# Threshold attention and SwiGLU on one core: one 130-column matmul for the last keys of both heads, score tiles with one user each at the end, stores on two queues

## The chip, the cores and the metric

The kernel runs on one core of a Trainium2 chip. A core has a matrix engine (TensorE, PE in the profile; its weight loads are PEld), a vector engine (VectorE, DVE), a scalar engine for activations (ScalarE, ACT), a general engine (GpSimd, POOL) and a queue engine (SyncE, SP) that here only issues transfers. They run side by side and wait for one another through semaphores. PE writes to PSUM, 8 banks of 128 partitions by 512 fp32 numbers; ACT and DVE read it from there; POOL does not. The metric is the time of one execution on the device in microseconds; the kernel before has a median of 575.13 us over six runs (574.01 to 576.0).

## The reference

Attention over 8 batches, 8 heads, 576 positions, head size 64, in which a score counts only if it lies within tau of the maximum of its row; then a gated feed-forward layer over the 4608 rows of 512.

```python
scores = scale * np.matmul(q, k.transpose(0, 1, 3, 2))
thresh = np.max(scores, axis=-1, keepdims=True) - tau
scores = np.where(scores >= thresh, scores, -1000000000.0)
scores = scores - np.max(scores, axis=-1, keepdims=True)
attn = np.exp(scores)
attn = attn / (np.sum(attn, axis=-1, keepdims=True) + 1e-09)
x = np.matmul(attn, v)                      # then heads side by side: 4608 x 512
...
rms = np.sqrt(np.mean(x * x, axis=-1, keepdims=True) + 1e-06)
xn = x / rms * rms_g
g = xn @ w_gate                             # 512 x 1536
silu = g * (1.0 / (1.0 + np.exp(-g)))
val = xn @ w_val
return (silu * val @ w_out).astype(np.float32)
```

## The kernel before

**Chunks and steps.** 128 query rows are a chunk. A batch of 576 rows gives four main chunks ("m"), and the 64 rows left over of two batches make one tail chunk ("v"): 36 chunks. A step is one chunk with one pair of heads, four steps a chunk, 144 in all. In a step PE computes the scores of both heads against 576 keys (line 566, into the two score tiles `s_ps[0]` and `s_ps[1]`, each of two PSUM banks), DVE copies them to `ssb` and takes the row maximum (line 589), POOL makes the threshold (line 596), ACT and POOL turn them into weights `wsb` (lines 607 to 645), and a transposing transfer on SP's queue (line 674; the first 16 steps go through PE, line 659) brings them as `wt`, nine blocks of 128 keys: four whole ones of head 0, one with the last 64 keys of head 0 and the first 64 of head 1, four of head 1. The sum over the values (`emit_av`, line 682, matmul at 696) takes two steps at a time: for each pair of heads, 5 matmuls a head, each of 65 columns, 64 of the values and one of ones for the row's sum of weights. The mixed block is used by both heads; the value tile `va` has rows of zeros there (entries 8 and 9, set at lines 270 and 271). In a tail chunk the upper and the lower 64 rows belong to two batches, so every matmul is made twice, with 64 columns of weights.

**The feed-forward layer.** DVE divides by the sum of weights (lines 712, 713) into `xsb`; ACT, POOL and a transposing transfer give the normalized, transposed chunk `xnT`. The chunks go through the layer in 12 groups (SIZES: four of two chunks, six of four, two of two). A group has 12 blocks of 128 hidden columns. For each, PE makes two products with the weights, g (line 790) and v (line 795), four matmuls each, of 512 columns in a group of four chunks and of 256 in a group of two; ACT takes tanh of g (line 804), DVE makes silu (line 807, frees g's tile) and the gate with v (line 812, `hf`, frees v's tile). Then the output sums: 12 matmuls of 512 columns a chunk. In eleven groups they come after the blocks, in two parts of six (line 849). In the last group (STREAMED = 1) they run between the blocks: one accumulation per chunk stays open over all 12 blocks, and each block adds two matmuls (line 829), planned OUT_LAG = 3 blocks behind its products. ACT evicts a finished sum to `osb` (line 863), in the last group DVE evicts the second chunk (line 861), and SP stores it (line 868; line 872 for a tail chunk).

**PSUM.** `ring` has four tiles of one bank and, as entries 4 to 7, the halves of the two score tiles: 4 and 5 are halves of `s_ps[0]`, 6 and 7 of `s_ps[1]` (line 207). Entries 4 to 7 join the ring only after the last scores have been read (`opens`, line 952). The framework puts waits between instructions that touch the same tile; a half of a score tile is the same tile as the other half.

**What sets the order.** Every piece of work is an `Op` with an engine, a planned cost (`COST`, line 16), a priority and what it needs. `order_ops` (line 42) plays them through with these costs, picks for each engine what can start first, gives out ring entries (those free first), and so fixes the order of each engine's instructions and the tiles they use. The costs decide the order alone; the chip then runs each engine's list in that order.

Of the kernel before, what the change touches and what calls it, by code (L numbers as in the profile page):

```python
# [13 lines left out]
SEM = 160.0  # L14
SLACK = 0.0
COST = dict(
    s_main=932.0, s_virt=900.0, tr_qk=530.0, tr4=230.0, tr_full=440.0, av_main=320.0, av_virt=500.0, ffn4=216.0, warm=3500.0,
    ttr=690.0, evac_qk=600.0, evac_half=380.0, evac_kt=350.0, prelu=700.0, exp2=1250.0, exp1=690.0, exp0=690.0,
    mask_d=750.0, mask_g=1740.0, take_g=1300.0, trw=510.0, evac_w=450.0, evac_wp=900.0, rz=180.0, xmul=420.0, sq=800.0, xn=720.0,
    pool_tiny=270.0, pool_mean=800.0, pool_dma=850.0, cast_v=650.0, cast_vt=420.0, cast_w=720.0,  # L20
# [4 lines left out]


class Op:
    __slots__ = ("eng", "cost", "prio", "deps", "fn", "ring", "frees", "slot", "end", "start", "dma", "opens", "nring", "mode", "bulk", "release")

    def __init__(self, eng, cost, prio, deps, fn, ring=None, frees=None, dma=0.0, nring=1, mode=0, bulk=False):  # L30
        self.eng, self.cost, self.prio, self.fn = eng, cost, prio, fn
        self.deps = [d for d in deps if d is not None]
        self.ring, self.frees, self.dma = ring, frees, dma
        self.slot = self.end = self.start = None
        self.opens = ()
        self.nring = nring
        self.mode = mode
        self.bulk = bulk
        self.release = 0.0


def order_ops(ops, ring_sizes):


    import heapq

    ring_free = {r: [(0.0, i) for i in range(n)] for r, n in ring_sizes.items()}
    users = {}
    left = {}
    for i, o in enumerate(ops):  # L50
        left[i] = len(o.deps)
        for d in o.deps:
            users.setdefault(id(d), []).append(i)
    pending = {}
    for i, o in enumerate(ops):
        pending.setdefault(o.eng, [])
        if not left[i]:
            pending[o.eng].append(i)
    eng_free = {e: 700.0 for e in pending}
    dma_free = 0.0  # L60
    mode = 0
    out = []
    ready_at = {i: 0.0 for i in range(len(ops))}
    while len(out) < len(ops):
        best = None
        for e, lst in pending.items():
            if not lst:
                continue
            t0 = eng_free[e]
            cand = None  # L70
            for i in lst:
                o = ops[i]
                t = max(t0, ready_at[i])
                if o.ring is not None:
                    if len(ring_free[o.ring]) < o.nring:
                        continue
                    t = max(t, sorted(ring_free[o.ring])[o.nring - 1][0])
                other = e == "PE" and o.mode != mode
                t = max(t, o.release)
                if o.bulk:  # L80
                    t = max(t, dma_free - BACKLOG)
                k = (t + (BIAS if other else 0.0), o.prio, i)
                if cand is None or k < cand:
                    cand = k
            if cand is not None and (best is None or cand < best[0]):
                best = (cand, e)
        (t, _, i), e = best
        o = ops[i]
        cost = o.cost
        if e == "PE":  # L90
            if o.mode != mode:
                t -= BIAS
                cost += SWITCH
            mode = o.mode
        o.start = t
        if o.ring is not None:
            o.slot = []
            for _ in range(o.nring):
                got = min(ring_free[o.ring])
                ring_free[o.ring].remove(got)  # L100
                o.slot.append(got[1])
        eng_free[e] = t + cost
        if o.dma:
            dma_free = max(dma_free, t + 300.0) + o.dma
            o.end = max(dma_free, t + o.cost) + (LAT_TR if o.cost == COST["sp_tr"] else 2000.0)
        else:
            o.end = t + cost
        if o.frees is not None:
            ring_free["R"].append((o.end + SEM, o.frees[0].slot[o.frees[1]]))
        for slot in o.opens:  # L110
            ring_free["R"].append((o.end + SEM, slot))
        pending[e].remove(i)
        out.append(o)
        for j in users.get(id(o), []):
            u = ops[j]
            wait = 0.0 if u.eng == o.eng and not o.dma else SEM + (SLACK if u.eng == "PE" else 0.0)
            ready_at[j] = max(ready_at[j], o.end + wait)
            left[j] -= 1
            if not left[j]:
                pending[u.eng].append(j)  # L120
    return out
# [3 lines left out]
def kernel(  # L125
# [12 lines left out]
    nc = tc.nc  # L138
    B, H, S, D = q.shape
# [78 lines left out]
    def add(eng, cost, prio, deps, fn, **kw):  # L218
        o = Op(eng, cost, prio, deps, fn, **kw)
        ops.append(o)  # L220
        return o
# [455 lines left out]
            w_read[s] = t  # L677
            w_ready[s] = [t]

    V_AT = ((0, 2, 4, 6, 8), (9, 1, 3, 5, 7))  # L680

    def emit_av(s):

        ci, p1 = steps[s]
        kind, b, c = chunks[ci]
        hp = p1 // 2

        def fn(o):
            for i in range(2):
                w, p = wt[(s - 1 + i) % NWT], p1 - 1 + i  # L690
                for h in range(2):
                    at = (2 * i + h) * (D + 1)
                    rows = [(slice(0, 128), b % 2)] if kind == "m" else [(HALF[e], e) for e in range(2)]
                    for rs, vi in rows:
                        for j in range(5):
                            nc.tensor.matmul(ring[o.slot[0]][rs, at:at + D + 1], w[:, 4 * h + j, rs],  # L696
                                             va[vi][:, p, V_AT[h][j]], start=(j == 0), stop=(j == 4))

        bs = [b] if kind == "m" else [2 * b, 2 * b + 1]
        deps = w_ready[s - 1] + w_ready[s] + [x for bb in bs for i in range(2) for x in v_ready[bb, p1 - i]]  # L700
        o = add("PE", 2 * COST["av_main" if kind == "m" else "av_virt"], s + AV_PRIO, deps, fn, ring="R",
                mode=0 if kind == "m" else 3)
        for i in range(2):
            av_of[s - i] = [o]
            for bb in bs:
                last_av[bb, p1 - i] = last_av.get((bb, p1 - i), []) + [o]

        r = rz[len(half_ev) % 3]

        def half(_):  # L710
            o3 = ring[o.slot[0]][:, 0:4 * (D + 1)].rearrange("p (h d) -> p h d", d=D + 1)
            nc.vector.reciprocal(out=r, in_=o3[:, :, D])
            nc.vector.tensor_tensor(  # L713
                out=xsb[ci % 2][:, 256 * hp:256 * hp + 256].rearrange("p (h d) -> p h d", d=D),
                in0=o3[:, :, 0:D], in1=r[:, :, None].to_broadcast([128, 4, D]), op=ALU.mult)

        half_ev.append(add("DVE", COST["rz"] + COST["xmul"], s + HALF_PRIO, [o] + x_done.get(ci - 2, []), half,
                           frees=(o, 0)))
# [48 lines left out]
    def emit_ffn(slot, parts, ready_step, pace, streamed):  # L767
# [55 lines left out]
        if streamed:  # L823

            acc = None
            for fc, (hi, m_) in enumerate(hs):
                def omm(o, fc=fc, hi=hi, first=acc):
                    for j in range(len(parts)):
                        nc.tensor.matmul(ring[(first or o).slot[j]], hf[hi][:, 128 * j:128 * (j + 1)], wo[:, fc],  # L829
                                         start=(fc == 0), stop=(fc == NFC - 1))  # L830

                mo = add("PE", len(parts) * COST["ffn4"], st + dt * (fc + OUT_LAG), [m_] + wo_ld + outs[-1:], omm,
                         ring=None if acc else "R", nring=len(parts))
                acc = acc or mo
                outs.append(mo)
                hf_use[hi] = [mo]
        for j, (ci, _) in enumerate(parts):
# [24 lines left out]
                else:  # L862
                    nc.scalar.activation(out=osb[oi], in_=ring[mo.slot[at]], func=AF.Copy, scale=0.5)  # L863

            def store(o, oi=oi, kind=kind, b=b, c=c):
                if kind == "m":
                    dst = out[b * S:b * S + MAIN].rearrange("(si sc) d -> si sc d", sc=4)[:, c]
                    nc.sync.dma_start(out=dst, in_=osb[oi])
                else:
                    for e in range(2):  # L870
                        r0 = (2 * b + e) * S + MAIN
# [1 line left out]

            e = add("DVE" if late else "ACT", 690.0 if late else 620.0, pr - PUSH[0], [outs[-1], osb_use.get(oi)], ev,
                    frees=(mo, at))
            osb_use[oi] = add("SP", COST["sp"] if kind == "m" else 1100.0, pr, [e], store, dma=DMA_NS['out'])
        if not streamed:
            for hi, _ in hs:
                hf_use[hi] = list(outs)
# [69 lines left out]
        if step > 0:  # L949
            o.deps.append(s_of[int(step)])  # L950
    for h in range(2):
        ttr_of[len(steps) - 1, h].opens = (4 + 2 * h, 5 + 2 * h)
    seq = order_ops(ops, {"R": 4})
    global LAST_SEQ
    LAST_SEQ = seq
# [3 lines left out]


PACE = 13.0
NHF = 16
SIZES = (2, 2, 2, 2, 4, 4, 4, 4, 4, 4, 2, 2)
LAG = 16.0
LAT_TR = 3000.0
REL = (0.0, 0.0)
REL_N = (0, 0)
STREAMED = 1
OUT_LAG = 3.0
OUT_PART = 6  # L970
ELAG = 16.0
NELAG = 0
# [58 lines left out]
```

## Time and profile before

| | |
|---|---|
| median of six runs | 575.13 us |
| the profiled execution | 575.72 us |
| its span, first to last instruction | 574.0 us |
| PE busy | 559.9 us (98%) |
| DVE, ACT, POOL busy | 426.8, 459.8, 322.6 us |
| scores, line 566, main chunks | 1024 matmul records, 171.4 us busy |
| value sums, line 696 | 1580 matmul records, 56.4 us busy |
| stores of 256 KB from SP | 32, median 2.7 us to landing |
| granted PE clock, mean | 0.999 of full |

Times are microseconds from the span's start. Matmuls overlap in the pipeline, so the records of one group add up to more than the time it adds; the chain of waits gives the advance. A chain line has start, length and what ran then; "issue" is time in which an engine waited for nothing that the profile shows. A line of stretches gives, per engine, busy time and in brackets the number of instructions. A line of groups gives line, engine, operation, output and inputs with shapes, count, busy time, mean length in ns, idle time just before and what ended it.

### The profile page before, as it was taken

What the parts mean: (1) busy time and instruction counts of PE and PEld (TensorE: products, weight loads), DVE (VectorE), ACT (ScalarE), POOL (GpSimd) and SP (SyncE); (2) the same over time, 40 slices, a digit from 0 to 9 for tenths busy, and PEclk for the clock granted to TensorE, in tenths of its full rate; (3) what the DMA queues carried; (4) which work ended last, traced back from release to release, by engine and by line L of the source; (5) the groups of instructions that cost most, each with busy time, mean ns of one, the idle gap of its engine ahead of it and who ended that gap; (6) DMA issues with size and microseconds to landing.
All of it is one profiled execution on the core that took longest, in us unless ns stands there. A gap on an engine that the chain in (4) does not pass through costs nothing.

```text
span 574.0 us, 14110 instructions
## 1 busy us (share of the span) xinstructions
PE 559.9 (98%) x5160; PEld 333.0 (58%) x5160; DVE 426.8 (74%) x1093; ACT 459.8 (80%) x739; POOL 322.6 (56%) x462
## 2 busy tenths in 40 slices
PE   8999999999999999999999999999999999999995
PEld 4666776767757555555555455655555455544763
DVE  4898986868848688659975889578867886585543
ACT  4998898998969788889988997888978997883322
POOL 2377956875747456655765666665666665541000
PEclk9999999999999999999999999999999999999999
DMA  8999999868995679988887597966788544641111
GB/s 183 233 262 242 237 180 204 149 133 193 176 184 120 131 159 153 175 163 186 154 190 159 119 173 172 196 162 148 164 199 164 108 102 112 146 93 48 56 38 37
DMA packets 271173, 89.01 MB, mean 155 GB/s; under 512 B 253696, under 2 KB 263424, under 8 KB 271104
## 3 DMA queue, kind: packets, MB, share of 16 engines
q1 hardware_dynamic: 268448, 86.28, 70.8%
q0 software_dynamic: 1600, 1.57, 1.8%
q8 instruction: 40, 0.66, 0.5%
q10 hardware_dynamic: 1056, 0.26, 0.2%
q14 instruction: 29, 0.24, 0.1%
HBM read 37.75 MB, written 9.44 MB: 82 GB/s over the span
## 4 chain that ended last, share of the span: by engine, by line
PE 85%; DVE 4%; DMA 4%; issue 2%; ACT 2%; POOL 1%; SPq 1%; DVEq 0%; POOLq 0%; ACTq 0%
PE s_ps L566 26%; PE ring L795 14%; PE ring L849 14%; PE ring L790 14%; PE ring L696 7%; PE ring L302 2%; DMA qkn<-in_q_dram 2%; DVE ssb L589 2%; PE s_ps L790 1%; DMA wt<-wsb 1%; PE s_ps L795 1%; DMA stage<-in_moe_w_gate_dram 1%; PE s_ps L829 1%; PE ring L364 1%; PE s_ps L849 1%
## 5 line engine op out<-in xcount | busy, mean ns | idle before, releaser
L589 DVE CUSTOM_DVE_ANT_0 ssb<-s_ps,zrow 128x576 f32<-128x576 f32 x288 | 206.8, 753 | 60.8 <-PE s_ps L566 55.7
L607 ACT ACTIVATE ssb<-ssb,nth 128x576 f32<-128x576 f32 x224 | 165.6, 766 | 26.4 <-POOL nth L596 26.0
L566 PE MATMUL s_ps<-qkt 64*128 64x288 f32 x1024 | 171.4, 430 | 1.6 <-DVE mx L589 1.4
L566 PEld LDWEIGHTS s_ps<-qkt 64*128 64x128 f32 x1024 | 95.7, 186 | 56.0 <-DVE mx L589 14.2
L640 POOL TENSOR_SCALAR wsb<-ssb,nth 128x576 f16<-128x576 f32 x64 | 110.5, 1726 | 13.0 <-ACT osb L863 5.0
L790 PE MATMUL ring<-xnT,wg 128*128 128x512 f16 (+1 forms) x524 | 108.4, 329 | 0.2 <-DVE sl L807 0.2
L795 PE MATMUL ring<-xnT,wv 128*128 128x512 f16 (+1 forms) x520 | 107.5, 329 | 0.2 <-DVE xsb L713 0.2
L596 POOL TENSOR_SCALAR nth<-mx 128x2 f32<-128x2 f32 x144 | 31.6, 220 | 131.4 <-DVE mx L589 117.3
L614 ACT ACTIVATE wsb<-ssb 128x1152 f16<-128x1152 f32 x80 | 93.0, 1163 | 2.5 <-DMA wt<-wsb 0.2
L849 PE MATMUL ring<-wo,hf 128*128 128x512 f16 x384 | 89.3, 380 | 0.0
L804 ACT ACTIVATE th<-ring 128x512 f32<-128x512 f32 (+1 forms) x131 | 63.6, 487 | 31.4 <-PE ring L790 25.9
L645 POOL TENSOR_TENSOR wsb<-wsb,esb 128x576 f16<-128x576 f16 x64 | 81.8, 1278 | 9.8 <-ACT esb L626 5.0
L807 DVE SCALAR_TENSOR_TENSOR sl<-th,ring 128x512 f32<-128x512 f32 (+1 forms) x131 | 72.9, 556 | 15.8 <-ACT th L804 15.3
L812 DVE TENSOR_TENSOR hf<-ring,sl 128x512 f16<-128x512 f32 (+1 forms) x130 | 73.0, 562 | 13.1 <-PE ring L795 4.6
L795 PEld LDWEIGHTS <-wv 128*128 128x128 f16 x576 | 51.7, 98 | 43.8 <-issue 14.4
L790 PEld LDWEIGHTS <-wg 128*128 128x128 f16 x576 | 52.1, 98 | 40.7 <-issue 10.6
L849 PEld LDWEIGHTS <-hf 128*128 128x128 f16 x408 | 37.4, 98 | 47.0 <-issue 6.6
L696 PEld LDWEIGHTS <-wt 128*128 128x128 f16 (+1 forms) x1600 | 51.6, 100 | 19.9 <-issue 9.8
L696 PE MATMUL ring<-va,wt 128*128 128x65 f16 (+1 forms) x1580 | 56.4, 194 | 1.4 <-DMA wt<-wsb 1.4
L626 ACT ACTIVATE esb<-ssb,nth 128x576 f16<-128x576 f32 x64 | 49.2, 769 | 5.1 <-POOL nth L596 4.7
L611 ACT ACTIVATE wsb<-ssb 128x576 f16<-128x576 f32 x64 | 43.6, 682 | 1.7
L713 DVE TENSOR_TENSOR xsb<-ring,rz 128x256 f32<-128x256 f32 x71 | 30.2, 425 | 2.5
(65 smaller groups left out, 419.4 us busy)
## 6 DMA issues: line engine op xcount, KB each, us to landing
vst<-in_v_dram SPq DMA_DIRECT2D x32, 256.0 KB, 3.2
out_dram<-osb SPq DMA_DIRECT2D x32, 256.0 KB, 2.7
qkn<-in_k_dram SPq DMA_DIRECT2D x62, 128.0 KB, 3.3
qkn<-in_q_dram SPq DMA_DIRECT2D x56, 128.0 KB, 3.1
stage<-in_moe_w_gate_dram SPq DMA_DIRECT2D x12, 256.0 KB, 4.6
stage<-in_moe_w_val_dram SPq DMA_DIRECT2D x12, 256.0 KB, 4.6
wt<-wsb SPq DMA_TRANSPOSE x128, 3.1
wo<-in_moe_w_out_dram POOLq DMA_DIRECT2D x4, 384.0 KB, 6.8
```

Of the source, the lines that this page charges most:

```text
L566: nc.tensor.matmul(s_ps[h][rows, ROW_AT + n * part:ROW_AT + n * part + n], lhs(hs), kT[i][p][h][hs, n * part:n * part + n], start=True, st ...
L589: nc.vector.tensor_tensor_reduce(out=ssb[a][:, h], in0=s_ps[h][:, ROW_AT:ROW_AT + S], in1=zrow, scale=-1.0 / 8.0, scalar=3.0e38, op0=ALU.a ...
L607: nc.scalar.activation(out=ssb[a][:, h], in_=ssb[a][:, h], func=PRELU, scale=-1.0, bias=nth[m][:, h:h + 1], **PRELU_KW)
L614: nc.scalar.activation(out=wsb[s % NW], in_=ssb[a], func=AF.Exp)
L640: nc.gpsimd.tensor_scalar(out=wsb[s % NW][:, h], in0=ssb[a][:, h], scalar1=nth[m][:, h:h + 1], scalar2=None, op0=ALU.is_le)
L645: nc.gpsimd.tensor_tensor(out=wsb[s % NW][:, h], in0=wsb[s % NW][:, h], in1=esb[es], op=ALU.mult)
L696: nc.tensor.matmul(ring[o.slot[0]][rs, at:at + D + 1], w[:, 4 * h + j, rs], va[vi][:, p, V_AT[h][j]], start=(j == 0), stop=(j == 4))
L790: nc.tensor.matmul(ring[o.slot[0]][:, 0:n], wg[d][:, fs], xnT[slot][:, d, 0:n], start=(d == 0), stop=(d == 3))
L795: nc.tensor.matmul(ring[o.slot[0]][:, 0:n], wv[d][:, fs], xnT[slot][:, d, 0:n], start=(d == 0), stop=(d == 3))
L807: nc.vector.scalar_tensor_tensor(out=sl[i][:, 0:n], in0=th[i][:, 0:n], scalar=1.0, in1=ring[g.slot[0]][:, 0:n], op0=ALU.add, op1=ALU.mult)
L812: nc.vector.tensor_tensor(out=hf[hi][:, 0:n], in0=ring[vv.slot[0]][:, 0:n], in1=sl[i][:, 0:n], op=ALU.mult)
L849: nc.tensor.matmul(ring[(first or o).slot[0]], hf[hs[fc][0]][:, 128 * j:128 * (j + 1)], wo[:, fc], start=(fc == 0), stop=(fc == NFC - 1))
```

## The change

In the value sum the mixed block is multiplied once, with the values of both heads side by side, 130 columns, and opens the accumulation of both heads; four blocks of 65 columns a head follow. The loop over the halves of a tail chunk moves outside the loop over heads. The planned costs of the step fall from 320 to 310 and from 500 to 480.

At the end, only one half of each score tile joins the ring (entries 4 and 6). An `Op` can carry `pick`, the ring entries it may take; the first output sum of the last group has `pick = ACC`, entries 4 and 6, for its two chunks. OUT_LAG goes from 3 to 5. The store of the second chunk of the last group is issued by ACT. The planned latency of bulk loads gets a name of its own (LAT_LD) with the value it had.

```diff
-    V_AT = ((0, 2, 4, 6, 8), (9, 1, 3, 5, 7))
...
-                for h in range(2):
-                    at = (2 * i + h) * (D + 1)
-                    rows = [(slice(0, 128), b % 2)] if kind == "m" else [(HALF[e], e) for e in range(2)]
-                    for rs, vi in rows:
-                        for j in range(5):
-                            nc.tensor.matmul(ring[o.slot[0]][rs, at:at + D + 1], w[:, 4 * h + j, rs],
-                                             va[vi][:, p, V_AT[h][j]], start=(j == 0), stop=(j == 4))
+                rows = [(slice(0, 128), b % 2)] if kind == "m" else [(HALF[e], e) for e in range(2)]
+                for rs, vi in rows:
+
+                    at = 2 * i * (D + 1)
+                    nc.tensor.matmul(ring[o.slot[0]][rs, at:at + 2 * (D + 1)], w[:, 4, rs],
+                                     va[vi][:, p, 8:10].rearrange("p e d -> p (e d)"), start=True, stop=False)
+                    for h in range(2):
+                        for j in range(4):
+                            nc.tensor.matmul(ring[o.slot[0]][rs, at:at + D + 1], w[:, 5 * h + j, rs],
+                                             va[vi][:, p, 2 * j + h], start=False, stop=(h == 1 and j == 3))
+                        at += D + 1
...
-    s_main=932.0, s_virt=900.0, tr_qk=530.0, tr4=230.0, tr_full=440.0, av_main=320.0, av_virt=500.0, ffn4=216.0, warm=3500.0,
+    s_main=932.0, s_virt=900.0, tr_qk=530.0, tr4=230.0, tr_full=440.0, av_main=310.0, av_virt=480.0, ffn4=216.0, warm=3500.0,
...
-                    if len(ring_free[o.ring]) < o.nring:
+                    free = [f for f in ring_free[o.ring] if o.pick is None or f[1] in o.pick]
+                    if len(free) < o.nring:
                         continue
-                    t = max(t, sorted(ring_free[o.ring])[o.nring - 1][0])
+                    t = max(t, sorted(free)[o.nring - 1][0])
...
-                got = min(ring_free[o.ring])
+                got = min(f for f in ring_free[o.ring] if o.pick is None or f[1] in o.pick)
...
-                acc = acc or mo
+                if not acc:
+
+                    acc, mo.pick = mo, ACC
...
-                    nc.sync.dma_start(out=dst, in_=osb[oi])
+                    (nc.scalar if late else nc.sync).dma_start(out=dst, in_=osb[oi])
...
-            osb_use[oi] = add("SP", COST["sp"] if kind == "m" else 1100.0, pr, [e], store, dma=DMA_NS['out'])
+            late = late and kind == "m"
+            osb_use[oi] = add("ACT" if late else "SP", COST["sp"] if kind == "m" else 1100.0, pr, [e], store,
+                              dma=DMA_NS['out'])
...
-        ttr_of[len(steps) - 1, h].opens = (4 + 2 * h, 5 + 2 * h)
+        ttr_of[len(steps) - 1, h].opens = OPENS[h]
...
+ACC = (4, 6)
+OPENS = ((4,), (6,))
...
-OUT_LAG = 3.0
+OUT_LAG = 5.0
```

More of the change, by code (lines that the diff above doesn't have):

```diff
@@ L27 @@
 class Op:
-    __slots__ = ("eng", "cost", "prio", "deps", "fn", "ring", "frees", "slot", "end", "start", "dma", "opens", "nring", "mode", "bulk", "release")
+    __slots__ = ("eng", "cost", "prio", "deps", "fn", "ring", "frees", "slot", "end", "start", "dma", "opens", "nring", "mode", "bulk", "release", "pick")
     def __init__(self, eng, cost, prio, deps, fn, ring=None, frees=None, dma=0.0, nring=1, mode=0, bulk=False):
@@ L39, in __init__ @@
         self.release = 0.0
+        self.pick = None
 def order_ops(ops, ring_sizes):
@@ L104, in order_ops @@
             dma_free = max(dma_free, t + 300.0) + o.dma
-            o.end = max(dma_free, t + o.cost) + (LAT_TR if o.cost == COST["sp_tr"] else 2000.0)
+            o.end = max(dma_free, t + o.cost) + (LAT_TR if o.cost == COST["sp_tr"] else LAT_LD if o.bulk else 2000.0)
         else:
@@ L863, in ev, with store @@
                     nc.scalar.activation(out=osb[oi], in_=ring[mo.slot[at]], func=AF.Copy, scale=0.5)
-            def store(o, oi=oi, kind=kind, b=b, c=c):
+            def store(o, oi=oi, kind=kind, b=b, c=c, late=late):
                 if kind == "m":
                     dst = out[b * S:b * S + MAIN].rearrange("(si sc) d -> si sc d", sc=4)[:, c]
-                    nc.sync.dma_start(out=dst, in_=osb[oi])
+                    (nc.scalar if late else nc.sync).dma_start(out=dst, in_=osb[oi])
                 else:
@@ L965 @@
 LAT_TR = 3000.0
+LAT_LD = 2000.0
 REL = (0.0, 0.0)
```

## The prediction, written before the changed kernel ran

> **What bounds the kernel now.** I read the busy times first: PE is busy for 559.9 of 574.0 us, DVE for 74% and ACT for 80%, so what can be won is PE's 14.1 us of idle time, or PE work taken out. The second view is the busy time of each engine by stretch, cut where the instruction order of the changed program first departs (88 us), where idle time nearly ends (180 us) and where the last group of four chunks begins its output sums (524 us).
>
> ```profile
> core 0: us, PE busy (x) PEld busy (x) DVE busy (x) ACT busy (x) POOL busy (x), PEclk, DMA share, GB/s
> 0.00:88.00 88.00, 82.96 (x824) 56.97 (x825) 69.98 (x200) 72.51 (x115) 50.63 (x93) 1.00 1.01 223
> 88.00:180.00 92.00, 90.08 (x954) 61.84 (x953) 70.90 (x201) 80.97 (x138) 61.47 (x84) 1.00 0.87 168
> 180.00:524.00 344.00, 343.66 (x3102) 186.15 (x3099) 264.09 (x641) 292.13 (x455) 209.06 (x284) 1.00 0.72 150
> 524.00:574.00 50.00, 43.17 (x290) 28.10 (x288) 21.79 (x53) 14.17 (x34) 1.45 (x3) 0.99 0.14 46
> ```
>
> The reader is to see the first number after the length: PE idles 5.0 us at the start (there the order is unchanged), 1.9 us to 180, 0.3 us in the long middle, 6.8 us in the last 50. Only the last stretch is large, and the chain of waits says why:
>
> ```profile
> 524.37 10.37 PE ring L849 x48
> 534.74 0.03 ACTq L863
> ...
> 535.74 0.60 PE s_ps L790 x4
> ...
> 545.89 5.19 PE s_ps L849 x24
> 551.09 0.02 issue
> 551.11 0.61 ACT osb L863
> 551.72 0.04 issue
> 551.76 0.60 PE s_ps L795 x4
> ...
> 554.54 0.45 PE s_ps L829 x2
> 554.99 0.02 issue
> 555.01 0.39 ACT th L804
> ...
> 555.42 0.43 DVE sl L807
> ...
> 555.95 0.44 DVE hf L812
> 556.39 0.04 issue
> 556.43 0.59 PE s_ps L829 x2
> ```
>
> The chain leaves PE in the middle of the last group: tanh of one block waits for an output sum (L829), and the next output sum waits for that block's silu and gate. They share no data. They share the tile s_ps: the sums lie in one half of s_ps0 and of s_ps1, the block's two products in the other halves. The same pattern returns at 559.2 and 563.9. At 551.1 a product waits for an eviction of the neighbouring half, at 535.7 for a tanh.
>
> **The change, part by part.** The sum is made against the profiled execution, span 574.0 us, its time 575.72 us; the 1.72 us outside the span are left as they are.
>
> (a) The 130-column matmul. On the 128-row chunks a weighted sum of one head pair goes from 10 matmuls of 65 columns to 8 of 65 and one of 130, with one weight load less. There are 64 such steps with two pairs, 128 mergers. Price: one step of 20 advances the chain by 0.61 us (at 85.39 us and in most others), 30.5 ns each. No 130-column row exists. The nearest are the 128-column transposes, and above them the 256-column products (0.44 us for 4 in the chain, 109 ns):
>
> ```profile
> 53.89 0.50 PE ring L659 x9
> ```
>
> 0.50 / 9 is 55.6 ns. On a line from 65 columns at 30.5 ns to 128 at 55.6 ns, 130 columns take 56.4 ns; I take this, two columns from the nearer row. A merger saves 61.0 - 56.4 = 4.6 ns, 128 of them 0.6 us. Ends: 55.6 ns gives 0.7 us gained, 109 ns would give 128 x 48 ns = 6.1 us lost, which so near to the 128-column row I leave out. The Trainium skill, "TensorE: Matmul & The Clock Gate", section "Back-to-back issue gap", speaks against the change: in a stream of weight load and matmul pairs it gives a sustained spacing of about 81 ns at 128 columns, not the 56 ns of a lone gap. By that figure, as an estimate, a merger would lose 81 - 61 = 20 ns, 2.6 us over 128. The row above has a weight load before each of its matmuls and advances by 55.6 ns, so the sum goes by the row.
>
> In the 8 steps on the tail chunk, 40 matmuls of 128x64 become 36, and their order changes: all nine of one half of the partitions, then all nine of the other, where five and five alternated. The group of that form shows 320 matmuls in 7.1 us, 22 ns each, less than the 30.5 ns of a full one, so the halves overlap today. If they go on overlapping, nothing changes (the columns are the same). If the longer blocks end the overlap, a step takes 32 x 30.5 + 4 x 56.4 = 1.20 us instead of 0.89 us: 2.5 us lost in all. I take 0, since they now overlap across blocks of five pairs. Part (a): -0.6 us.
>
> (b) One user for each score tile, the group before the last. It now takes its products from the four ring tiles and one half of each score tile. In the program as built no product writes beside a half that is being read. From the end of the sums, 534.74, to 545.89 the chain shows 11.15 us; the work is 24 groups of four at 0.436 us (0.44 in the chain), 10.46 us. The difference, 0.69 us, goes. The tanh before 535.7 still waits for ACT's last eviction, but PE has three tile pairs to go on with, 2.6 us of work. Six tiles in place of eight are enough: from the start of a block's first product to the end of its gate is 2.0 to 2.4 us in this stretch. -0.7 us.
>
> (c, d) The last group. From 551.08 to PE's end at 569.39 are 18.31 us. The work is 24 x 0.436 + 24 output matmuls at 0.216 to 0.218 (1.31 us for 6) = 15.7 us. So 2.6 us are waits: 0.4 us at 551.1, and three times 0.73 us (1.44 us of the chain from 554.99 to 556.43, less the 0.87 us of two products done meanwhile, plus 0.16 us because the next L829 starts at 0.59 instead of 0.43). The sums now lie alone in their tiles, and products use the four ring tiles. A ring tile comes round after two blocks, 2 x 1.30 us of PE work, against the 2.0 to 2.4 us above, so no new wait there. Sums trail by five blocks (OUT_LAG 5): after the last product five pairs of output matmuls follow, 2.2 us, of which 1.7 us cover the last gate (0.2 drain + 0.42); at present three pairs do. New is one wait: the first sum needs both score tiles back, so the gate of block five. It is placed 13 groups, 5.67 us, into the stage; that gate ends 5.5 to 5.9 us in (start at 3.49 us, plus 2.0 to 2.4). Behind it all of PE is queued; cost 0 to 0.45 us with the 0.16 us restart, I take 0.1. -2.6 + 0.1 = -2.5 us.
>
> (e) The last store goes from SP's queue to ACT's. DVE's eviction, which starts at 569.41 and takes 0.69 us, ends at 570.10; SP issues that store only at 570.58, after its other one of 569.82:
>
> ```profile
> 570.58 0.33 SPq L868 DMA_DIRECT2D out_dram<-osb  x1
> ```
>
> On ACT nothing stands ahead of it (its eviction ends at 569.79) and nothing is queued behind. SP's first store was issued 0.03 us after its eviction; the same on ACT gains 0.45 us. The transfers then overlap more: the first took 2.1 us to landing, the second 2.5. If both share a fixed rate the gain is 0; if the second also takes 2.1 us it is 0.8; ACT's two loads at the start took 0.64 us to issue, which could cost 0.3. I take -0.45, ends -0.8 to +0.3. The Trainium skill, "DMA: Bandwidth & Descriptors", section "Issuing engines are not separate DMA queues", says that several issuers save only the sequencer's time to initiate. By it the gain would be the 0.33 us of the row, 0.1 us less than taken.
>
> (f) The order. The planned costs of L696's steps fall (320 to 310, 500 to 480), and from 88 us on 337 of PE's 652 steps stand elsewhere, by at most 8 places; SP's queue moves by up to 6. Both orders go 137 times from full-array work to scores and 104 times straight back, so the price of switching is the same. PE's idle 1.9 us in 88 to 180 can vanish or double: 0, ends -1.9 to +1.9.
>
> Sum: -0.6 - 0.7 - 2.5 - 0.45 = -4.25 us, a span of 569.75 us. The median of the runs, 575.13 us, is 0.6 us under the profiled 575.72; taken from it: **570.9 us**.
>
> **The rivals.**
> 1. The waits move instead of going. During the sums only four tiles serve the products, and DVE (0.42 + 0.42 us a block) can be late with them. For it: in the group before, DVE is busy 8.18 of 11.00 us, and the slack at the first sum is about nothing. Against: with sums a block costs PE 1.30 us and DVE 0.84. If the three waits stay, 2.2 us come back: 573.1 us.
> 2. The tail chunk's halves stop overlapping: +2.5 us, 573.4 us. For it: blocks of nine. Against: the 22 ns row.
> 3. Slower: the new order uses up PE's reserve in the middle. Between 180 and 524 us ACT is 85% and DVE 77% busy and PE idles 0.1%, because products stand ready between score steps. Scores wait for DVE already (in 88 to 180 the weight loads of L566 waited 2.9 us for it, 10 times). If the middle idled like that stretch, 2.1%, it would lose 7.2 - 0.3 = 6.9 us: 577.8 us. It decides from 1.2% of 344 us on, which eats the 4.25. Against: the displacements are small and the switches equal.
> 4. A milder form of 3, or several ends at once, leaves about 575.
>
> **How the numbers follow.** Forecast 0.66, own range 568.8 to 573.0 (the ends of the first sum's wait, e and f, about 0.4, 0.7 and 1.9 us, put together as squares: 2.1 us). Rival 1: 0.11, rival 2: 0.07, rival 4: 0.07, rival 3: 0.09. About 0.2%, 1.15 us, is what a measurement can tell. Faster is the forecast with rivals 1 and 2, less a little for their upper edges: 0.82; same 0.09, slower 0.09. The range of 568.8 to 574.0 leaves out rivals 3 and 4 and a little below.
>
> **What would show it.** In the profile after, the last group should have no pieces of ACT or DVE between L829's successors; output sums to PE's end about 15.8 us; the stretch before it 10.5 us; the last store on ACT's queue within 0.1 us of its eviction; L696's step of 18 at 0.59 us; PE idle of about 0.3 us in the middle. Wrong it is if the middle idles by several us, if the tail chunk's steps take 1.2 us, or if the first sum waits longer than 0.5 us.

## The result, and the profile after

The changed kernel takes 572.89 us (median of 40 runs, 570.62 to 576.55), the kernel before beside it 574.61 us (82 runs, 572.51 to 578.01). The ratio is 0.997, 95% interval 0.9961 to 0.998: 1.7 us faster, where 4.25 us were forecast. The profiled execution took 573.62 us, its span is 571.5 us. Two of the 21 executions of the kernel before in the first set of experiments took 1873 us; the ratios leave them out, and without them its median there is 574.83 us.

The busy time by stretch, in the columns of the prediction:

```profile
core 0: us, PE busy (x) PEld busy (x) DVE busy (x) ACT busy (x) POOL busy (x), PEclk, DMA share, GB/s
0.00:88.00 88.00, 82.64 (x803) 56.73 (x803) 69.79 (x199) 72.35 (x115) 50.43 (x92) 1.00 1.02 223
88.00:180.00 92.00, 90.20 (x938) 62.63 (x935) 71.86 (x203) 81.29 (x139) 63.05 (x86) 1.00 0.83 168
180.00:524.00 344.00, 343.70 (x2972) 188.10 (x2971) 264.54 (x640) 291.84 (x455) 207.23 (x282) 1.00 0.73 150
524.00:571.50 47.50, 43.09 (x295) 28.63 (x293) 21.77 (x53) 13.83 (x33) 1.44 (x3) 1.00 0.14 48
```

PE idles 5.4, 1.8, 0.3 and 4.4 us, where it was 5.0, 1.9, 0.3 and 6.8: the middle is as full as before, and the 4.4 us of the end are all behind PE's last matmul. So waits did go, and the rest of the gain must have been spent in work that counts as busy. The chain of waits shows where:

```profile
101.73 0.54 PE ring L794 x4
102.27 0.17 PE ring L695
102.45 0.16 PE ring L699 x5
102.60 0.03 PE ring L695
102.64 0.18 PE ring L699 x7
102.82 0.03 PE ring L695
102.85 0.18 PE ring L699 x7
103.03 0.03 PE ring L695
103.06 0.27 PE ring L699 x10
103.33 0.54 PE ring L799 x4
...
122.36 0.06 PE ring L695
122.42 0.24 PE ring L699 x8
122.66 0.06 PE ring L695
122.72 0.24 PE ring L699 x8
...
525.41 5.18 PE ring L855 x24
530.59 5.18 PE s_ps L855 x24
535.77 0.44 PE ring L794 x4
...
546.25 5.18 PE ring L855 x24
551.43 0.44 PE ring L794 x4
...
557.11 0.86 PE s_ps L833 x4
557.97 0.44 PE ring L799 x4
...
564.93 2.17 PE s_ps L833 x10
567.11 0.02 issue
567.13 0.69 DVE osb L867
```

L695 is the 130-column matmul, L699 the 65-column one, L794 and L799 the two products, L855 and L833 the output sums. Three things are to be seen.

- The first block is a value sum on a tail chunk. It lasts from 102.27 to 103.33, 1.06 us; before, the same step took 0.81 us (below). By the starts of the matmuls that follow, the eight such steps took 0.814 to 0.819 us before and 1.063 to 1.070 after: 2.0 us lost.
- A value sum on a main chunk, at 122.36, advances by 0.06 + 0.24 us for each pair of heads, 0.60 us, where it was 0.61. By starts, the steps go from 0.621 to 0.609 us (median, those between a score matmul, which uses 64 rows of the array, and one of all 128) and from 0.704 to 0.690 (before scores). Over 64 steps some 0.75 us are gained.
- From the sums of the group before the last on, no ACT or DVE piece stands between PE's pieces until DVE's last eviction. From the start of those sums to PE's end are 567.09 - 525.41 = 41.7 us, where they were 569.39 - 524.37 = 45.0 us: 3.3 us gained.

The lines of the kernel before that these stand against, from its chain: a value sum on a main chunk, one on a tail chunk (the chain names 28 of its 40 matmuls, since they overlap; the time is that between the neighbours), and PE's end:

```profile
85.39 0.61 PE ring L696 x20
...
101.46 0.54 PE ring L790 x4
102.00 0.81 PE ring L696 x28
102.82 0.54 PE ring L795 x4
...
568.08 1.31 PE s_ps L829 x6
569.39 0.02 issue
569.41 0.69 DVE osb L861
```

### The profile page after: what moved, and what is told of

Its sections match the earlier page's. It is cut to its first block, busy times and chain, and to the rows that moved or that the text cites. A ratio compares the mean times of both kernels' runs of the same rounds, so it can differ in the third digit from the quotient of the medians.

```text
span 571.5 us, 13800 instructions
## 1 busy us (share of the span) xinstructions
PE 559.6 (98%) x5000; PEld 336.1 (59%) x5000; DVE 428.0 (75%) x1093; ACT 459.3 (80%) x739; POOL 322.2 (56%) x462
## 4 chain that ended last, share of the span: by engine, by line
PE 90%; DMA 4%; DVE 2%; SPq 1%; ACT 1%; issue 1%; POOL 1%; ACTq 0%; DVEq 0%; POOLq 0%
PE s_ps L568 28%; PE ring L799 16%; PE ring L794 16%; PE ring L855 15%; PE ring L699 6%; PE ring L304 2%; DMA qkn<-in_q_dram 2%; PE ring L695 2%; DVE ssb L591 1%; PE s_ps L794 1%; PE s_ps L833 1%; PE s_ps L855 1%; DMA stage<-in_moe_w_val_dram 1%; SPq L294 1%; PE s_ps L799 1%
## 5 line engine op out<-in xcount | busy, mean ns | idle before, releaser
L799 PE MATMUL ring<-xnT,wv 128*128 128x512 f16 (+1 forms) x544 | 111.8, 328 | 0.6 <-DVE xsb L717 0.5
L794 PE MATMUL ring<-xnT,wg 128*128 128x256 f16 (+1 forms) x540 | 110.9, 328 | 0.0
L811 DVE SCALAR_TENSOR_TENSOR sl<-th,ring 128x512 f32<-128x512 f32 (+1 forms) x135 | 74.6, 552 | 28.8 <-ACT th L808 28.3
L808 ACT ACTIVATE th<-ring 128x512 f32<-128x512 f32 (+1 forms) x135 | 65.3, 485 | 31.3 <-PE ring L794 26.6
L855 PE MATMUL ring<-wo,hf 128*128 128x512 f16 x384 | 89.3, 380 | 0.0
L816 DVE TENSOR_TENSOR hf<-ring,sl 128x512 f16<-128x512 f32 (+1 forms) x136 | 76.2, 560 | 12.6 <-PE ring L799 2.9
L794 PEld LDWEIGHTS <-wg 128*128 128x128 f16 x576 | 51.3, 98 | 44.8 <-issue 15.9
L799 PEld LDWEIGHTS <-wv 128*128 128x128 f16 x576 | 52.8, 98 | 40.4 <-issue 9.0
L855 PEld LDWEIGHTS <-hf 128*128 128x128 f16 x408 | 37.5, 98 | 47.1 <-issue 6.2
L699 PE MATMUL ring<-va,wt 128*128 128x65 f16 (+1 forms) x1264 | 52.8, 193 | 0.0
L699 PEld LDWEIGHTS <-wt 128*128 128x128 f16 (+1 forms) x1280 | 48.7, 100 | 3.9
L695 PE MATMUL ring<-va,wt 128*128 128x130 f16 (+1 forms) x158 | 35.1, 227 | 0.0
```

The lines of the kernel that those rows point to most:

```text
L699: nc.tensor.matmul(ring[o.slot[0]][rs, at:at + D + 1], w[:, 5 * h + j, rs], va[vi][:, p, 2 * j + h], start=False, stop=(h == 1 and j == 3))
L794: nc.tensor.matmul(ring[o.slot[0]][:, 0:n], wg[d][:, fs], xnT[slot][:, d, 0:n], start=(d == 0), stop=(d == 3))
L799: nc.tensor.matmul(ring[o.slot[0]][:, 0:n], wv[d][:, fs], xnT[slot][:, d, 0:n], start=(d == 0), stop=(d == 3))
L811: nc.vector.scalar_tensor_tensor(out=sl[i][:, 0:n], in0=th[i][:, 0:n], scalar=1.0, in1=ring[g.slot[0]][:, 0:n], op0=ALU.add, op1=ALU.mult)
L816: nc.vector.tensor_tensor(out=hf[hi][:, 0:n], in0=ring[vv.slot[0]][:, 0:n], in1=sl[i][:, 0:n], op=ALU.mult)
L855: nc.tensor.matmul(ring[(first or o).slot[0]], hf[hs[fc][0]][:, 128 * j:128 * (j + 1)], wo[:, fc], start=(fc == 0), stop=(fc == NFC - 1))
```

## The experiments

A kernel is named by its label. Times are medians, with the ratio to the kernel before as run beside it (574.83, 575.24 and 575.04 us in the three sets) and its 95% interval. The ratio is not the quotient of the two medians: for alt that would be 0.994, and 0.9925 is on record. "Outside the span" is the time of an execution less its span. Angle brackets in the cuts of code stand for the matmul calls of the diff above.

### The order of the halves in a tail chunk

**alt**: as the changed kernel, but each matmul of one half is followed by the same of the other.

```diff
-                for rs, vi in rows:
-                    <wide matmul>
-                    for h in range(2):
-                        for j in range(4):
-                            <65-column matmul>
+                for rs, vi in rows:
+                    <wide matmul>
+                for h in range(2):
+                    for j in range(4):
+                        for rs, vi in rows:
+                            <65-column matmul>
```

> The changed kernel with the loop over the two halves of a tail chunk moved innermost, so that the halves alternate matmul by matmul; order of steps, tiles and stores as in the changed kernel. Theory A (the blocks of nine cost the overlap of the halves, 1.066 us a tail-chunk step instead of 0.814, 8 steps): the step falls to about 0.8 us and the time to 2.0 us under the changed kernel's, about 570.9 beside 574.6 of the kernel before. Theory B (the step's length is hidden or the loss of about 1 us before the end stage comes from the new order of PE's steps): the time stays within 0.7 us of the changed kernel's 572.9.

Measured: 571.29 us, 0.9925 (0.99 to 0.9951); the step takes 0.743 us. A tail step of its chain:

```profile
104.15 0.54 PE ring L794 x4
104.69 0.18 PE ring L694 x2
104.87 0.25 PE ring L699 x16
105.12 0.06 PE ring L694 x2
105.18 0.25 PE ring L699 x16
105.43 0.54 PE ring L799 x4
```

Sixteen matmuls of half the array advance by 0.25 us, the time of eight full ones (0.24): the halves now run wholly side by side, and a step costs little more than one on a main chunk. The wide matmul is therefore not what made the tail step long.

**block18** and **block5** change the length of a block of one half: all 18 matmuls of a half, or 5 and 4 in turn.

```diff
 block18
-            for i in range(2):
-                for rs, vi in rows:
+            for rs, vi in rows:
+                for i in range(2):
 block5
-                for rs, vi in rows:
-                    for h in range(2):
+                for h in range(2):
+                    for rs, vi in rows:      # the wide matmul at h == 0
```

> The changed kernel with blocks of 18 matmuls per half in a tail-chunk step (both pairs of one half, then both of the other). If the overlap of the halves is lost by the length of a block: a step of 1.15 to 1.25 us, near the 1.20 us of no overlap at all. If only the wide matmul spoils it: 1.07 us as in blocks of nine.

> The changed kernel with the halves alternating in blocks of five and four (wide matmul and head 0 of one half, of the other, head 1 of one, of the other). If the length of a block decides: a step of 0.74 to 0.85 us, as with blocks of five before. If the wide matmul spoils the overlap: about 1.07 us.

Measured, one run each: block18 574.99 us, step 1.262 us; block5 570.71 us, step 0.827 us. The chain of block18 at the same step:

```profile
102.28 0.17 PE ring L694
102.46 0.25 PE ring L698 x8
102.71 0.06 PE ring L694
102.77 0.16 PE ring L698 x5
102.92 0.03 PE ring L694
102.96 0.27 PE ring L698 x10
103.23 0.06 PE ring L694
103.29 0.25 PE ring L698 x8
103.54 0.54 PE ring L798 x4
```

The chain is in order of start, and the counts tell how far the overlap reaches (of the 36 matmuls it leaves out one, in the x10). The third L694 opens the other half. It starts after five of the eight matmuls ahead of it: three of the first half are still to come and run beside it. In the changed kernel the second L695 starts after five of eight likewise. So at each change of half the next block gets ahead by about three matmuls, some 0.09 us at 30 ns each, and no further. A step has one change with blocks of 18, three with blocks of nine, seven with blocks of five, and 35 when they alternate; it takes 1.26, 1.07, 0.83 and 0.74 us. Why the reach is three matmuls stays open.

**av_alone** and **before_alt**: the kernel before with only the new value sums, in the changed kernel's order of halves and in alt's. Costs, tiles, lag and stores are those of before.

```diff
 av_alone, in the kernel before
-                for h in range(2):
-                    for rs, vi in rows:
-                        for j in range(5):
-                            <65-column matmul>
+                for rs, vi in rows:
+                    <wide matmul>
+                    for h in range(2):
+                        for j in range(4):
+                            <65-column matmul>
 before_alt, in the kernel before
+                for rs, vi in rows:
+                    <wide matmul>
+                for h in range(2):
+                    for j in range(4):
+                        for rs, vi in rows:
+                            <65-column matmul>
```

> The kernel before with the new value-sum matmuls alone; planned costs, order, tiles at the end and stores as before. Theory A: 64 main steps 0.011 us shorter each (-0.7 us), 8 tail-chunk steps 0.25 us longer (+2.0 us), so 1.3 us slower than the kernel before, about 575.9 us. Theory B: the value sums are a small gain, 0.7 us faster, about 573.9 us.

> The kernel before with only the value sums of the changed kernel, but with the tail chunk's halves alternating matmul by matmul. Theory: the 130-column matmul is worth what the main chunks show (64 steps by about 0.012 us, 0.75 us) and the alternation 8 x (0.814 - 0.743) = 0.57 us more, so 1.3 us under the kernel before: ratio 0.997 to 0.999, where av_alone, which differs in the order of the halves alone, had 1.0012. Rival: the wide matmul brings nothing to the time of the whole, since a PE that is done sooner waits longer for ACT and DVE in the middle: ratio 1.000, with PE's idle time between 180 and 524 us grown by about 1 us.

Measured: av_alone 576.18 us, 1.0012 (0.9992 to 1.0032), tail step 1.063 to 1.070 us, main step before scores 0.690 us. before_alt 574.02 us, 0.9978 (0.9956 to 1.0), and PE is busy for all of 180 to 524 us. By the steps the first should lose 2.0 - 0.75 = 1.25 us and the second gain 0.75 + 8 x (0.814 - 0.743) = 1.3 us. By the medians of their sets the first is 1.35 us slower and the second 1.0 us faster; the first interval still reaches no change and the second ends there, so the sizes rest on the traces.

### The end

**end_alone**: the changed kernel with the old value sums and the old planned costs, that is, the tiles, the lag and the store alone. **lag3**: the same with the lag of three. **shared5**: the same with the lag of five, but the score tiles shared again.

```diff
 end_alone: emit_av of the kernel before; av_main=320.0, av_virt=500.0
 lag3, beside that
-OUT_LAG = 5.0
+OUT_LAG = 3.0
 shared5, beside end_alone
-ACC = (4, 6)
-OPENS = ((4,), (6,))
+ACC = (0, 1, 2, 3, 4, 5, 6, 7)
+OPENS = ((4, 5), (6, 7))
```

> The changed kernel with the value sums and their planned costs as before, so that the order up to the last groups is as before: one user per score tile, lag 5 and the store on ACT's queue alone. Theory A: PE's end 3.3 us earlier and 0.2 us from the store, 3.1 to 3.6 us faster than before, about 571.2 us; the three waits of ACT and DVE in the chain of the last group are gone. Theory B (the end's gain is partly given back later): 1.7 us faster, about 572.9 us.

> The kernel of end_alone (old value sums, new end) with the sums of the last group trailing by three blocks instead of five. It parts the two edits at the end: tiles of one user, and the lag. Theory: the tiles bring the gain and the lag only covers the last gate. Then the stretch from the start of the group of four's sums to PE's end is 41.7 us plus up to 0.6 us (three pairs of output sums, 1.3 us, against some 1.9 us from the last product's end to the next output sum's start), 41.7 to 42.4 us, no wait comes back at the three places of before, and the time is 571.6 to 572.2 us. Rival: the lag brings the gain, as the tanh of a block and the sums beside it are only kept apart by it; then the three waits of 0.73 us come back, 43.9 us and 573.8 us.

> The kernel of end_alone with the score tiles shared again (two products' tiles in each, sums free to take any ring tile) and the lag of five kept. Theory (a shared tile makes the waits): the waits between output sums and tanh or gate come back, as in before: three of about 0.73 us and 0.4 to 0.7 us in the group before, a stretch of 43.9 to 45.0 us, a time of 573.8 to 574.9 us. Rival (the lag brings it): 41.7 to 42.4 us, 571.6 to 572.3 us.

| | time, us | ratio (95%) | sums of the group before to PE's end |
|---|---|---|---|
| end_alone | 571.58 | 0.9934 (0.991 to 0.9957) | 523.13 to 564.81: 41.7 us |
| lag3 | 571.01 | 0.9941 (0.992 to 0.9961) | 522.36 to 564.04: 41.7 us |
| shared5 | 574.14 | 0.9987 (0.9963 to 1.0011) | 521.70 to 565.11: 43.4 us |

With tiles of their own the lag makes no difference, not even behind the last product, where lag3 expected up to 0.6 us (its time, too, lies under the 571.6 to 572.2 us that it expected). With shared tiles the lag of five brings 1.6 of the 3.3 us, more than expected; the waits come together at fewer places:

```profile
532.64 0.39 ACT th L806
533.03 0.04 issue
533.07 0.60 PE s_ps L792 x4
...
552.34 0.61 PE s_ps L792 x4
...
554.80 0.34 DVE sl L809
...
555.23 0.42 DVE hf L814
```

The tanh and the silu between PE's pieces are back in both groups. In shared5 the sums could also go to the four ring tiles, and did (its L831 lines name `ring`), so part of the 1.6 us may be that choice and not the lag. The tiles with one user suffice for the whole gain.

### The store and the planned costs

**store_sp**: the changed kernel with its last store on SP's queue again. **alt_costs** and **new_costs** part the planned costs, which only set the order, from the value sums: alt with the old costs, and end_alone with the new ones.

```diff
 store_sp
-                    (nc.scalar if late else nc.sync).dma_start(out=dst, in_=osb[oi])
+                    nc.sync.dma_start(out=dst, in_=osb[oi])
 alt_costs, in alt
-av_main=310.0, av_virt=480.0
+av_main=320.0, av_virt=500.0
 new_costs, in end_alone
-av_main=320.0, av_virt=500.0
+av_main=310.0, av_virt=480.0
```

> The changed kernel with the last store back on SP's queue. If the store on ACT's queue gains what the profiles say between PE's end and the end of the span (4.39 us against 4.61), the span is 0.2 us longer and the time about 573.1 us. If the use of ACT's queue is what makes the time outside the span 2.12 us instead of 1.72, the time outside returns to 1.72 us and the time is about 572.7 us. The prediction's 0.45 us would give 573.35.

> The kernel with alternating halves, its planned costs of the value sums put back to 320 and 500, so that PE's steps keep the order of the kernel before up to the end stage. Theory A (end -3.3 us, main mergers -0.7, tail-chunk steps at 0.743 us -0.6): 4.6 us faster than the kernel before, about 570.3 us, and about 0.4 us outside the span less than in the changed kernel, 1.78 in place of 2.15 us, if that goes with the order. Theory B (the new order gains or loses in the middle by itself): the time differs from the alternating kernel's 571.3 us by more than 1.0 us either way.

> The end changes with the old value sums, but with planned costs 310 and 480: the new order alone, beside the same kernel in the old order (571.6 us). Theory A: the middle is neutral, so within 0.7 us of 571.6; if the 0.37 us outside the span goes with the new order, it is 2.15 us here too and the time about 572.0 us. Theory B: the new order costs the 1.0 us that the changed kernel's profile shows before 525 us: about 572.6 us or more.

store_sp: 572.87 us, 0.9962 (0.9942 to 0.9982), the changed kernel's time. The timeline of the changed kernel's ACT shows the issue where it was meant to be:

```profile
567.85 0.35 ACTq L874 DMA_DIRECT2D out_dram<-osb  x1
```

It follows DVE's eviction, which ends at 567.82, by 0.03 us. But the landing comes 2.76 us after that eviction, where it is 2.93 us before and 2.47 us in store_sp. In store_sp SP issues its second store 0.15 us after the eviction, where it took 0.47 us in before, av_alone and before_alt: in the changed kernel SP would hardly have been late. And an earlier issue does not bring the data earlier. In the changed kernel's trace the first store's packets run from 568.37 to 569.19 and the second's from 569.04 to 569.98: they begin 1.19 us after their issue, the first's 0.84 us after theirs. In all nine traces with the store on ACT the second's packets begin 0.15 to 0.17 us before the first's end.

From PE's end to the span's end are 4.4 us after, 4.6 before, 4.1 in store_sp; with the time outside the span, 6.5, 6.3 and 6.3 us. So these traces give the store on ACT a loss of some 0.2 us, and the runs cannot tell it from nothing (intervals of about 0.2%, 1.1 us, to either side).

alt_costs: 571.35 us, 0.9934 (0.9912 to 0.9957), against alt's 0.9925. new_costs: 571.0 us, 0.9928 (0.9907 to 0.9948), against end_alone's 0.9934. The new order is worth nothing that these runs can tell.

alt_costs misses its 570.3 us by 1.0 us. It differs from end_alone in the value sums alone, and lies 0.2 us below it where the steps promise 1.3; alt and new_costs differ likewise, and alt lies 0.3 us above. In the traces the value sums from the first tail step to the last take 34.5 us in alt and 35.9 in new_costs, but the transposes of the inputs, which stand in the same stretch and follow loads, take 13.7 and 12.2 there, and 12.0 to 14.1 across eleven kernels, whatever their value sums (each by the starts of the matmuls that follow). So the shorter steps are shown, and that the time of the whole gets shorter by them, beside the new end, is not: six runs a kernel leave over 1 us open.

One thing goes with the planned costs. Outside the span lie 2.08 to 2.22 us in every execution of a kernel with the new costs (the changed one, alt, store_sp, new_costs, block5, block18), and 1.72 to 1.84 us with the old (before, av_alone, before_alt, end_alone, lag3, shared5, alt_costs). It lies behind the last instruction: semaphores are still set 2.25 us after it in the changed kernel's trace and 1.90 us in that of before.

In all 13 traces it goes with the loads of 8 KB of instructions (queue q14 of the profile). With the old costs the last of them falls into the last store's data (571.50 in before, the store's packets run from 571.45 to 572.58), and none follows the last instruction. With the new costs it begins just as the store's data end (569.97 in the changed kernel), and one more begins 1.6 to 1.9 us behind the last instruction (573.33). The last store on ACT lands 2.70 to 2.74 us after its issue with the new costs, 3.12 to 3.21 with the old. No run moves these loads alone, so that they make the difference is not shown. It is no loss, though. alt and alt_costs, which differ in the planned costs alone, spend 4.38 + 2.16 = 6.54 and 4.81 + 1.75 = 6.56 us from PE's end to the end of the execution, new_costs and end_alone 6.56 and 6.61: what is longer behind the last instruction is shorter ahead of it.

The best kernels, alt, new_costs, block5 (one run), lag3, alt_costs and end_alone, lie between 570.7 and 571.6 us and cannot be told apart. alt's interval (0.99 to 0.9951) lies wholly below the changed kernel's (0.9961 to 0.998): the change with its halves alternating beats both kernels.

## Why the prediction was right or wrong

The direction and the range were right: 572.89 us lies in 568.8 to 574.0. The gain was 1.7 us of 4.25. That the range held is in part luck: it was made from the ends of the first sum's wait, the store and the order, and the step that failed was not among them. Point by point:

- **(a), main chunks: right by the steps, a little small.** The 130 columns advance by 0.06 us in the chain, as taken from the transposes; the steps give 0.75 us for the forecast 0.6. In the time of the whole it is not seen apart from the rest (alt_costs, alt). The Trainium skill, "TensorE: Matmul & The Clock Gate", section "Back-to-back issue gap", spoke for a loss with its spacing of about 81 ns at 128 columns in pairs of weight load and matmul; the main chunks' steps do not show that spacing, and the row decided rightly.
- **(a), tail chunks: the failed step.** "I take 0, since they now overlap across blocks of five pairs." The step takes 1.07 instead of 0.81 us, 2.0 us in all (the 0.89 us that the prediction starts from, 40 matmuls at 22 ns, is 0.81 by starts). The 22 ns row was a mean over blocks of five; it showed that halves overlap, but not how far. The reach is about three matmuls at each change of half, enough for most of a block of five and for a third of a block of nine. This is rival 2, given 0.07, at four fifths of its price (1.20 us a step without any overlap, as it was worked out; what remained is the overlap at the three changes, against a first wide matmul of 0.17 us that the price had left out). The rival was named, priced nearly right, and put aside on a row that was measured at another block length.
- **(b): right.** From the end of the sums to the next sums are 546.25 - 535.77 = 10.48 us, 0.67 less than the 11.15 before; 0.69 was forecast.
- **(c, d): right in size, half wrong in what does it.** 567.09 - 551.43 = 15.66 us from the output sums to PE's end; 15.8 were forecast with 0.1 us for the first sum's wait, which did not come (557.11 follows without a gap). The lag of five was taken as cover for the last gate; lag3 needs none.
- **(e): mis-sized.** "I take -0.45, ends -0.8 to +0.3": the runs of store_sp and the changed kernel show no difference, and the traces a loss of about 0.2 us from PE's end to the end of the execution. The issue came early as forecast; the data of the second store still began only as the first's ended, near the end that the step had named ("if both share a fixed rate the gain is 0"), and SP's own issue would have come only 0.15 us after the eviction. The Trainium skill, "DMA: Bandwidth & Descriptors", section "Issuing engines are not separate DMA queues", would have given at most the issuing time; the runs give less than that.
- **(f): right at 0 for the order.** Rival 3 did not come: PE idles 0.3 us in the middle as before. That "the 1.72 us outside the span are left as they are" did not hold: they are 2.1 with the new order; but the span's end gets shorter by as much, and the sum is unmoved.

The sum of the measured terms: -0.75 + 2.0 - 3.3 + 0.2 = -1.85 us, against the 1.7 us of the runs (interval 1.1 to 2.2); the 0.2 is from PE's end to the end of the execution, 6.53 us in place of 6.30, in one execution each. The forecast missed by 2.6 us: the tail step's 2.0 and the store's 0.65, less some 0.25 that the main chunks, (b) and the last group gave beyond their forecast; what is left is less than the runs can tell.

Rivals 1 and 3 and the mild rival 4 are refuted by the chain: no wait came back at the end, no idle time in the middle.

## What to carry to other kernels

A mean time per instruction that lies below the full price shows that work overlaps, not how far: when an edit changes the grouping, find in the trace where the second stream starts against the first, and price the new grouping by that reach. Where two halves of the array can work side by side, alternate them instruction by instruction. Two users of one tile wait for each other even when they touch different halves; giving each user a tile removed three waits and more, and needed no other tuning.

## What the runs showed of the hardware

- Matmuls of 128x64 on the two halves of the array overlap fully when they alternate (0.743 us for 36, where a main chunk's 18 full ones take 0.60 to 0.70), and by about three matmuls at each change of half otherwise (0.827, 1.066 and 1.262 us with blocks of 5 and 4, 9, and 18). The Trainium skill, "TensorEngine Tiling (Array Packing)", section "Key Properties", says that different tiles can execute weight loads and matmuls in parallel; the runs agree, and add that the order of issue decides how much of it is had.
- A second store of 256 KB, issued on another queue 0.3 us after the first, began to move its data only 0.15 to 0.17 us before the first's were through, in nine traces. It landed 2.70 to 2.74 us after its issue, and 3.12 to 3.21 where a load of 8 KB of instructions fell into its data.
- The time that an execution spends behind its last instruction differed by 0.4 us between kernels that differ only in the order of instructions; it was the longer one where one more load of 8 KB of instructions began behind the last instruction. The time from PE's end to the end of the execution stayed the same (6.54 and 6.56 us, 6.56 and 6.61).
- Single executions differ: alt's profiled one took 573.66 us, the longest of its six runs. Its granted PE clock was 0.96 over the first 88 us, where the changed kernel's was 1.00, and its PE is busy for 81.3 of them, where the changed kernel's is for 82.6. Positions in two traces are therefore compared stretch by stretch, from a common event on.
